# One transfer of queries a tile instead of two, in a windowed attention with two mixtures of experts behind it

## The chip, the cores and the metric

The kernel runs on one core of a Trainium2 chip. The metric is the device time in microseconds: before the change 337.52 us, the median of 3 runs (336.28 to 339.29).

A core has five engines that run side by side: TensorE (PE, matrix products, with its weight loads listed as PEld), VectorE (DVE), ScalarE (ACT), GpSimd (POOL) and SyncE (SP). SP computes nothing here: it issues transfers between the chip's memory (HBM) and the core's own memory of 128 partitions, and waits on semaphores before it issues. The transfers themselves are carried out by 16 DMA engines.

## The reference

Three stages follow one another. Batch 8, 8 heads, 576 positions, head size 64; the experts see 4608 rows of 512.

```python
scores = scale * np.matmul(q, k.transpose(0, 1, 3, 2))
mask_plain = (rel >= 0) & (rel < window)                                      # heads 0 to 3, window 32
mask_dil = (rel >= 0) & (rel < window * dilation) & (rel % dilation == 0)     # heads 4 to 7, dilation 4
attn = softmax(np.where(masks, scores, -1e9)); x = np.matmul(attn, v)
...
logits = x @ phi; d = softmax(logits, axis=0); slot_input = d.T @ x           # 32 slots, 8 experts
slot_out = relu(slot_input @ w1[e]) @ w2[e]; x = softmax(logits, axis=1) @ slot_out
...
e = argmax(x @ w_gate); out = gate * (relu(x @ m1[e]) @ m2[e])                # one expert a row
```

## The kernel before

The host lays out the inputs so that the dilated heads become plain ones: their positions are sorted by the remainder of 4. Every head then needs a window of at most 32 keys back, and a tile of 128 queries looks at its own 128 keys and the 32 before them.

The attention runs over 36 tiles (NTILE) of 128 queries, all 8 heads at once. Heads go in 4 groups `p`, and in each group two heads `hh` share the 128 partitions: head size 64 times 2 heads, interleaved, so that partition 2d + hh holds element d of head hh. `qt[t]` is `[128, 4, 128]` float32: partition, group, query. In HBM a tile's queries are 128 rows of 4 x 128 numbers (2 KB): first the 64 rows of hh = 0, then the 64 rows of hh = 1. `load` (lines 155 to 165) fetches them with two transfers of 64 rows, one to the even and one to the odd partitions (line 159), and the keys with two more (line 161) into `kt[r]`, in which the rows of one head are zero where the other head's keys stand; each row of 2 KB goes to four places of 512 B there. GpSimd then copies the last 32 keys of the tile before to the front (line 163). `load_v` (lines 174 to 185) fetches the values of a tile, 64 rows of 4160 B in each of two transfers (line 185). `load_w_part` (lines 109 to 122) fetches a part of an expert's weights, 512 KB in one transfer of 128 rows (lines 117 and 119); `prefetch` (line 127) spreads 28 of these parts over the attention's steps.

A step `s` of the loop (lines 490 to 519) sends to SP, in this order: at most one weight part as a rule, then `load(s + 2)`, which is q, q, k, k, then `load_v(s - 1)`, which is v, v. On PE a step holds the scores of tile s (`qk`, line 198, `s_ps`), the transposes of the probabilities of an earlier tile (`tr`, line 242, `a_ps`), the products with the values (`pv`, line 263, `x_ps`), the transposes of the result (`xt`, line 290), and in some steps the logits and the slot sums (`b_sl`, line 418, `sl_ps`). The first tiles' order is written out by hand (`HEAD`), and so is the end (`TAIL`). The scores of a tile need its q and both transfers of its k.

`q` and `kt` have two buffers each. So the q of tile t + 2 may be fetched only when PE has done the scores of tile t, and SP, which handles its list strictly in order, holds everything behind it meanwhile. Transfers from SP also share eight landing semaphores (DMAHW0 to DMAHW7 in the lists below) in rotation: an issue waits until the transfer eight places before it, which used the same semaphore, has landed.

After the attention come the rest of the weights for the experts, page by page as pages come free, and the two expert stages.

Of the kernel before, what the change touches and what calls it, by code (L numbers as in the profile page):

```python
# [73 lines left out]
def kernel_body(ctx, tc, q, k, v, mask, cpack, dk, rk, w1, w2, m1, m2, out):  # L74
    nc = tc.nc
# [22 lines left out]
    with tc.manual_schedule(), ExitStack() as ab:  # L98
# [34 lines left out]
        with ExitStack() as a:  # L133
# [19 lines left out]
            qt = {}  # L153

            def load(t):
                r = t % NR
                qt[t] = qp.tile([128, 4, 128], FP32, tag="q", name="q")
                for hh in range(2):
                    nc.sync.dma_start(out=qt[t][hh:128:2], in_=q[t, 64 * hh:64 * hh + 64])  # L159
                for hh in range(2):  # L160
                    nc.sync.dma_start(out=kt[r][hh:128:2, hh, :, WIN:], in_=k[t, hh])  # L161
                if t > 0:
                    nc.gpsimd.tensor_copy(  # L163
                        out=kt[r][:, :, :, 0:WIN], in_=kt[1 - r][:, :, :, 128:128 + WIN]
                    )
# [8 lines left out]
            def load_v(t):  # L174
                if t == NTILE - 2:
                    for i in range(NR):
                        for hh in range(2):
                            nc.sync.dma_start(
                                out=keys_as_values(i)[hh:128:2, hh],
                                in_=v[t, hh, :, 2 * i:2 * i + 2].rearrange("k p j c -> k (p j c)"),  # L180
                            )
                    return
                r = value_slot(t)
                for hh in range(2):
                    nc.sync.dma_start(out=vt[r][hh:128:2, hh], in_=v[t, hh])  # L185
# [7 lines left out]
            def qk(t, where="s", eng=nc.gpsimd):  # L193
                r = t % NR
                ps = psums[where].tile([128, 4, 64, 2], FP32, tag=where, name="s_ps")
                for p in range(4):
                    for j in range(4):
                        nc.tensor.matmul(  # L198
                            out=ps[32 * j:32 * j + 32, p].rearrange("q k h -> q h k"),
                            lhsT=qt[t][:, p, 32 * j:32 * j + 32],  # L200
                            rhs=kt[r][:, :, p, 32 * j:32 * j + 64],
                            start=True,
                            stop=True,
                        )
                del qt[t]
                s = sp.tile([128, 4, 64, 2], FP32, tag="s", name="s")
                first, step = MASKS[t % 9]
                for a in range(2):
                    nc.vector.tensor_tensor(  # L209
                        out=s[:, 2 * a:2 * a + 2],  # L210
                        in0=ps[:, 2 * a:2 * a + 2],
                        in1=mask_sb[:, first + a * step].unsqueeze(1).unsqueeze(3).to_broadcast([128, 2, 64, 2]),
                        op=ALU.add,
                    )
                mx = sm.tile([128, 4, 2], FP32, tag="mx", name="mx")
                nc.vector.tensor_reduce(out=mx, in_=s.rearrange("p a k h -> p a h k"), op=ALU.max, axis=AX.X)  # L216
                eng.tensor_tensor(  # L217
                    out=s, in0=s, in1=mx.unsqueeze(2).to_broadcast([128, 4, 64, 2]), op=ALU.subtract
                )
                s_sb[t] = s  # L220
# [162 lines left out]
            def b_order(b, engs="a"):  # L383

                n = 4 // len(engs)
                for k, eng in enumerate(engs):
                    r = slice(n * k, n * k + n)
                    o = lt_sb[b][:, 2, :].rearrange("p (r i) -> p i r", r=4)[:, :, r]
                    i = lt_sb[b][:, 1, :].rearrange("p (i r) -> p i r", r=4)[:, :, r]
                    copy(eng, o, i)  # L390
# [84 lines left out]
            def once(c, t, f, *o):  # L475
# [7 lines left out]
                c=lambda t: nc.sync.dma_start(out=cp_sb, in_=cpack), o=lambda t: nc.vector.memset(on_sb, 1.0),  # L483
                l=load, v=load_v, X=ex, r=tr, p=pv, x=xt,
                q=lambda t, w="s", e="g": qk(t, w, nc.gpsimd if e == "g" else nc.vector),
# [4 lines left out]
            for s in range(NTILE - 1):  # L490
# [16 lines left out]
                t = s - 4  # L507
# [20 lines left out]
            def b_lz(b):  # L528

                lt_sb[b] = tp.tile([128, 3, S], FP32, tag="lt", name="lt", bufs=1)  # L530
                mz = sm.tile([128, 2], FP32, tag="mz", name="mz", bufs=1)
                for c in range(2):
                    ps = lz_ps[c] = ps_m.tile([128, 288], FP32, tag="m", name="lt_ps")
                    nc.tensor.matmul(
                        out=ps, lhsT=is_sb, rhs=l4_sb[b][:, 288 * c:288 * c + 288], start=True, stop=True
                    )
                    nc.vector.tensor_reduce(out=mz[:, c:c + 1], in_=ps, op=ALU.max, axis=AX.X)
                mn = sm.tile([128, 1], FP32, tag="mn", name="mn")
                nc.vector.scalar_tensor_tensor(
                    out=mn, in0=mz[:, 0:1], scalar=m_run[0], in1=mz[:, 1:2], op0=ALU.max, op1=ALU.max  # L540
                )
                ng = sm.tile([128, 1], FP32, tag="ng", name="ng")
                nc.vector.tensor_scalar(out=ng, in0=mn, scalar1=-1.0, scalar2=None, op0=ALU.mult)
                ng_sb[b] = ng

            def b_ez(b):
                lt, ng = lt_sb[b], ng_sb[b]
                fac[b] = sm.tile([128, 1], FP32, tag="fac", name="fac")
                for c in range(2):
                    nc.scalar.activation(  # L550
                        out=lt[:, 1, 288 * c:288 * c + 288], in_=lz_ps[c], func=ACTF.Exp, bias=ng, accum_out=zb2[:, c:c + 1]
                    )
                nc.scalar.activation(out=fac[b], in_=m_run[0], func=ACTF.Exp, bias=ng)

            def b_zz(b):
                for c in range(2):
                    nc.scalar.activation(
                        out=zsum, in_=zsum, func=ACTF.Identity, scale=1.0 if c else fac[b], bias=zb2[:, c:c + 1]
                    )
                nc.scalar.activation(out=zsum, in_=zsum, func=ACTF.Copy, bias=1e-9)  # L560

            def b_isz():
                nc.vector.reciprocal(out=zsum, in_=zsum)
                nc.scalar.activation(out=isz, in_=is_sb[:, 0:NSLOT], func=ACTF.Copy, scale=zsum)

            def b_keep(b):
# [8 lines left out]
                q=lambda n, o: qk(last), v=lambda n, o: load_v(last - n),  # L575
# [6 lines left out]
                t=lambda n, o: b_lz(z), e=lambda n, o: b_ez(z), o=lambda n, o: b_order(z, *o),  # L582
                d=lambda n, o: b_dt(z, (n, n + 1)), z=lambda n, o: b_zz(z), i=lambda n, o: b_isz(),
# [11 lines left out]
            for h in range(2):  # L595
                o = slice(256 * h, 256 * h + 256)
                nc.vector.scalar_tensor_tensor(
                    out=acc[:, o], in0=acc[:, o], scalar=fac[z], in1=ps[:, o], op0=ALU.mult, op1=ALU.add
                )
                for c in (2 * h, 2 * h + 1):  # L600
                    nc.tensor.matmul(
                        out=si_ps[:, c], lhsT=acc[:, 128 * c:128 * c + 128], rhs=isz, start=True, stop=True
                    )
            nc.vector.tensor_copy(
                out=sm_sb.rearrange("p c (e x) -> p c e x", x=36)[:, :, :, 0:SPE],
                in_=si_ps.rearrange("p c (e s) -> p c e s", s=SPE),
# [22 lines left out]
        for p in late:  # L629
# [15 lines left out]
            out=csum[:, 0], in_=c_sb.rearrange("p t s -> p s t"), op=ALU.add, axis=AX.X  # L645
# [6 lines left out]
            out=isw[:, NSLOT:2 * NSLOT], in0=is_sb[:, 0:NSLOT], scalar1=-1.0 / NSLOT, scalar2=None, op0=ALU.add  # L652
# [84 lines left out]
        for e in range(E):  # L737
            for c in range(4):
                for j in range(4):
                    nc.tensor.matmul(  # L740
                        out=h_ps[32 * j:32 * j + 32, :],
# [25 lines left out]
        for hf in range(2):  # L767
            nc.vector.tensor_copy(
                out=hm_sb[:, hf].rearrange("p j (e x) -> p j e x", x=36)[:, :, :, 0:SPE],
                in_=ht_ps[:, hf].rearrange("p (j e s) -> p j e s", j=4, s=SPE),  # L770
# [5 lines left out]
        for e in range(E):  # L776
            for fc in range(8):
                g = fc % 4
                nc.tensor.matmul(  # L779
                    out=so_ps[32 * g:32 * g + 32, :],  # L780
# [41 lines left out]
        for c in range(4):  # L822
            nc.tensor.matmul(
                out=lb_ps, lhsT=xm[:, c:c + 1], rhs=wg_sb[:, c], start=(c == 0), stop=(c == 3)
# [16 lines left out]
        for c in range(4):  # L841
            for a in range(4):
                nc.tensor.matmul(
                    out=g_ps[32 * a:32 * a + 32, :], lhsT=st_sb[:, c], rhs=wg_sb[:, c], start=(c == 0), stop=(c == 3)
# [7 lines left out]
            out=gbd[:, 0:4], in0=g_ps.unsqueeze(1).to_broadcast([128, 4, E]), in1=bm_sb, op=ALU.mult  # L852
# [12 lines left out]
        for b in range(9):  # L865
            nc.tensor.matmul(
                out=lg_w[:, 4 * b:4 * b + 12, :], lhsT=ct(b), rhs=gbd, start=True, stop=True
# [36 lines left out]
        def small(name, shape, dtype=FP32):  # L904
# [26 lines left out]
            out=trd_bf, in0=id_sb, scalar=1664.0, in1=tri_sb, op0=ALU.mult, op1=ALU.add  # L931
# [312 lines left out]
        def pick(k):  # L1244
# [10 lines left out]
            a=across, m=mixed_of, p=pick, h=halved,  # L1255
# [79 lines left out]
        with tc.If(nrest > 0):  # L1335
            rest(tc, dict(
                out=out, rk=rk, rev_sb=rev_sb, wes=wes, eq=eq, wm=wm, on_sb=on_sb, c_sb=c_sb, gate=gate,
# [377 lines left out]
```

## Time and profile before

| | before |
|---|---|
| median of 3 runs | 337.52 us (336.28 to 339.29) |
| profiled execution: time, span of the core | 340.81 us, 339.0 us |
| busy, share of the span: PE, DVE, ACT, POOL | 82%, 61%, 49%, 25% |
| transfers in total | 87.53 MB, mean 258 GB/s |
| q transfers | 72 of 128 KB, median 4.8 us from issue to landing |
| k transfers | 72 of 128 KB, 4.3 us |
| v transfers | 70 of 260 KB, 4.7 us |
| weight parts (w) | 72 of 512 KB, 6.3 us |

All rows of the profile come from one profiled execution, whose time is a little above the median. "Busy" leaves out the issuing of transfers, so SP has no busy time; it shows as SPq in the chain of work. The chain follows the work that ended last back from the end, at each step to what released it.

### The profile page before, as it was taken

What the parts mean: (1) busy time and instruction counts of PE and PEld (TensorE: products, weight loads), DVE (VectorE), ACT (ScalarE), POOL (GpSimd) and SP (SyncE); (2) the same over time, 40 slices, a digit from 0 to 9 for tenths busy, and PEclk for the clock granted to TensorE, in tenths of its full rate; (3) what the DMA queues carried; (4) which work ended last, traced back from release to release, by engine and by line L of the source; (5) the groups of instructions that cost most, each with busy time, mean ns of one, the idle gap of its engine ahead of it and who ended that gap; (6) DMA issues with size and microseconds to landing.
All of it is one profiled execution on the core that took longest, in us unless ns stands there. A gap on an engine that the chain in (4) does not pass through costs nothing.

```text
span 339.0 us, 10076 instructions
## 1 busy us (share of the span) xinstructions
PE 278.5 (82%) x3977; PEld 192.2 (57%) x3977; DVE 207.6 (61%) x512; ACT 164.6 (49%) x379; POOL 84.3 (25%) x139
## 2 busy tenths in 40 slices
PE   2677768998789889779787889899977778999992
PEld 1555556665665656556555535544463346888871
DVE  4645537868768687586867865532028866357760
ACT  1114537565574674474844841222113485187752
POOL 4023233222522324322223003930003343000000
PEclk9959999999999999999999999999999997999998
DMA  5878899998998989999989899999567020367654
GB/s 150 269 248 260 269 318 320 279 318 278 294 337 263 297 275 298 310 294 326 302 280 310 283 364 318 384 386 386 194 205 292 2 79 14 85 149 268 245 217 161
DMA packets 53954, 87.53 MB, mean 258 GB/s; under 512 B 5584, under 2 KB 26320, under 8 KB 53904
## 3 DMA queue, kind: packets, MB, share of 16 engines
q1 hardware_dynamic: 53520, 86.06, 76.8%
q0 software_dynamic: 384, 0.79, 0.9%
q8 instruction: 33, 0.54, 0.6%
q14 instruction: 17, 0.14, 0.1%
HBM read 77.39 MB, written 9.44 MB: 256 GB/s over the span
## 4 chain that ended last, share of the span: by engine, by line
PE 45%; DMA 24%; DVE 13%; SPq 10%; issue 4%; POOL 1%; ACT 1%; POOLq 0%; DVEq 0%
DMA kt<-in_k_dram 12%; PE o_ps L1169 9%; DMA vt<-in_v_dram 7%; DMA pg<-in_moe_w_dram 5%; PE s_ps L198 5%; PE so_ps L779 4%; PE sl_ps L418 4%; PE x_ps L263 4%; SPq L159 3%; SPq L161 3%; SPq L185 3%; PE o_ps L1162 2%; DVE trb L402 2%; PE a_ps L242 2%; PE cs_ps L724 1%
## 5 line engine op out<-in xcount | busy, mean ns | idle before, releaser
L198 PE MATMUL s_ps<-kt,q 128*32 128x128 f32 x1152 | 42.3, 291 | 31.8 <-DMA kt<-in_k_dram 28.1
L198 PEld LDWEIGHTS s_ps<-kt,q 128*32 128x32 f32 x1152 | 33.0, 116 | 40.2 <-issue 28.3
L217 POOL TENSOR_TENSOR s<-s,mx 128x512 f32<-128x512 f32 x33 | 34.5, 1044 | 77.6 <-DVE mx L216 39.6
L209 DVE TENSOR_TENSOR s<-s_ps,mask_sb 128x256 f32<-128x256 f32 x72 | 27.1, 417 | 30.6 <-PE s_ps L198 28.1
L263 PE MATMUL x_ps<-vt,at 128*32 128x130 f32 x1120 | 39.1, 279 | 7.5 <-DMA vt<-in_v_dram 7.3
L237 ACT ACTIVATE l<-l_ps 64x128 f32<-64x128 f32 (+4 forms) x100 | 24.1, 287 | 35.5 <-PE l_ps L319 35.1
L263 PEld LDWEIGHTS x_ps<-vt,at 128*32 128x32 f32 x1120 | 29.8, 109 | 13.7 <-issue 10.6
L1169 PE MATMUL o_ps<-pg,pg 128*128 128x512 f32 x132 | 36.9, 395 | 0.0
L1169 PEld LDWEIGHTS o_ps<-pg,pg 128*128 128x128 f32 x132 | 25.0, 190 | 6.5 <-issue 0.8
L224 ACT ACTIVATE e<-s 128x512 f32<-128x512 f32 x36 | 22.4, 623 | 11.6 <-DVE s L217 10.6
L237 ACT ACTIVATE at<-a_ps 128x512 f32<-128x512 f32 x34 | 20.3, 598 | 13.2 <-PE a_ps L242 12.4
L237 ACT ACTIVATE xt<-t_ps 128x512 f32<-128x512 f32 x36 | 21.4, 594 | 10.3 <-PE t_ps L290 10.1
L278 DVE TENSOR_TENSOR x<-x_ps,rec 128x512 f32<-128x512 f32 (+1 forms) x38 | 25.2, 663 | 1.3
L216 DVE TENSOR_REDUCE mx<-s 128x8 f32<-128x512 f32 x36 | 24.8, 688 | 1.2
L242 PE MATMUL a_ps<-cp_sb,e 128*128 128x128 f32 x144 | 24.9, 298 | 0.7 <-ACT e L224 0.7
L290 PE MATMUL t_ps<-cp_sb,x 128*128 128x128 f32 x144 | 23.4, 284 | 0.5 <-DVE den L273 0.5
L402 DVE STREAM_TRANSPOSE trb<-lt 32x480 f32<-32x480 f32 (+3 forms) x48 | 22.5, 468 | 1.7 <-ACT lt L550 1.2
L163 POOL COPY kt<-kt 128x256 f32<-128x256 f32 x35 | 13.9, 398 | 34.2 <-DMA kt<-in_k_dram 32.8
L1118 ACT ACTIVATE pg<-o_ps,gm 128x512 f32<-128x512 f32 x22 | 15.0, 689 | 12.5 <-PE o_ps L1169 12.2
L242 PEld LDWEIGHTS a_ps<-cp_sb,e 128*128 128x128 f32 x144 | 16.0, 147 | 8.2 <-PE s_ps L198 5.2
L290 PEld LDWEIGHTS t_ps<-cp_sb,x 128*128 128x128 f32 x144 | 15.6, 140 | 7.7 <-issue 5.6
L418 PE MATMUL sl_ps<-x,trb 128*32 128x256 f32 (+1 forms) x160 | 18.4, 390 | 0.0
(264 smaller groups left out, 440.9 us busy)
## 6 DMA issues: line engine op xcount, KB each, us to landing
pg<-in_moe_w_dram SPq DMA_DIRECT2D x72, 512.0 KB, 6.3
vt<-in_v_dram SPq DMA_DIRECT2D x70, 260.0 KB, 4.7
q<-in_q_dram SPq DMA_DIRECT2D x72, 128.0 KB, 4.8
kt<-in_k_dram SPq DMA_DIRECT2D x72, 128.0 KB, 4.3
out_dram<-pg SPq DMA_DIRECT2D x28, 256.0 KB, 2.1
out_dram<-pg SPq DMA_DIRECT2D x16, 128.0 KB, 2.3
kt<-in_v_dram SPq DMA_DIRECT2D x4, 130.0 KB, 6.5
dk_sb<-in_dk_dram SPq DMA_DIRECT2D x1, 370.5 KB, 10.3
```

The source lines that it names most:

```text
L198: nc.tensor.matmul(out=ps[32 * j:32 * j + 32, p].rearrange("q k h -> q h k"), lhsT=qt[t][:, p, 32 * j:32 * j + 32], rhs=kt[r][:, :, p, 32 ...
L209: nc.vector.tensor_tensor(out=s[:, 2 * a:2 * a + 2], in0=ps[:, 2 * a:2 * a + 2], in1=mask_sb[:, first + a * step].unsqueeze(1).unsqueeze(3 ...
L216: nc.vector.tensor_reduce(out=mx, in_=s.rearrange("p a k h -> p a h k"), op=ALU.max, axis=AX.X)
L217: eng.tensor_tensor(out=s, in0=s, in1=mx.unsqueeze(2).to_broadcast([128, 4, 64, 2]), op=ALU.subtract)
L237: nc.scalar.activation(out=out, in_=in_, func=ACTF.Copy)
L242: nc.tensor.transpose(ps[:, p], e_sb[t][:, p], id_sb)
L263: nc.tensor.matmul(out=ps[32 * j:32 * j + 32, p // 2 - sl.start, o:o + 2 * VW], lhsT=at_sb[t][:, p, 32 * j:32 * j + 32], rhs=vt[r][:, :, p ...
L278: nc.vector.tensor_tensor(out=x_sb[t][:, sl], in0=pv4[:, :, :, 0:HD], in1=rec.to_broadcast([128, n, 4, HD]), op=ALU.mult,)
L290: nc.tensor.transpose(ps[:, p], xf[:, p * 128:(p + 1) * 128], id_sb)
L402: nc.vector.transpose(out=tr_sb[b // 2][p0:p0 + 32, ws[0]:ws[1], i0:i0 + n, :], in_=src)
L418: nc.tensor.matmul(out=ps[32 * g:32 * g + 32, 256 * w:256 * w + 256], lhsT=tr_sb[b // 2][r0:r1, 1 + w, t % 9, :], rhs=xf[r0:r1, 256 * w:25 ...
L1169: nc.tensor.matmul(out=outs[b, i], lhsT=l[:, 128 * i:128 * i + 128], rhs=r, start=False, stop=(c == last and m == len(xs[b, c]) - 1),)
```

## The change

The two transfers of 64 rows become one of 128 rows. On the side of the core's memory it fills the partitions 0, 1, 2, ... in order; on the HBM side its rows come alternately from the first and the second half of the tile's 128 rows (d outside, h inside). The same bytes end in the same places. The key transfers stay two.

```diff
             def load(t):
                 r = t % NR
                 qt[t] = qp.tile([128, 4, 128], FP32, tag="q", name="q")
-                for hh in range(2):
-                    nc.sync.dma_start(out=qt[t][hh:128:2], in_=q[t, 64 * hh:64 * hh + 64])
+                nc.sync.dma_start(
+                    out=qt[t].rearrange("p a c -> p (a c)"), in_=q[t].rearrange("(h d) a c -> d h (a c)", h=2)
+                )
                 for hh in range(2):
                     nc.sync.dma_start(out=kt[r][hh:128:2, hh, :, WIN:], in_=k[t, hh])
```

Only SP's list changes. In the loop, a tile's share of that list with a weight part ahead and behind, before the change (a row is one issue: line, what it writes and reads, rows and shape, and the semaphores it waits on; the number behind a name is a buffer's):

```order
L117 DMA pg_543<-in_moe_w_dram 128x1024 [waits DMAHW6_49]
L159 DMA q<-in_q_dram 64x512 [waits DMAHW7_49,PE_49]
L159 DMA q<-in_q_dram 64x512 [waits DMAHW0_49]
L161 DMA kt_117<-in_k_dram 64x4x128 [waits DMAHW1_49,Pool_49]
L161 DMA kt_117<-in_k_dram 64x4x128 [waits DMAHW2_49]
L185 DMA vt_118<-in_v_dram 64x1040 [waits DMAHW3_49,PE_49]
L185 DMA vt_118<-in_v_dram 64x1040 [waits DMAHW4_49]
L117 DMA pg_543<-in_moe_w_dram 128x1024 [waits DMAHW5_49]
L159 DMA q<-in_q_dram 64x512 [waits DMAHW6_49,PE_49]
```

The last row's q waits on DMAHW6, which is the semaphore of the weight part in the first row. The same place in SP's list after the change (lines behind the edit stand one further down, those ahead of it are the same):

```order
L117 DMA pg_534<-in_moe_w_dram 128x1024 [waits DMAHW5_49]
L158 DMA q<-in_q_dram 128x1x512 [waits DMAHW6_49,PE_49]
L162 DMA kt_117<-in_k_dram 64x4x128 [waits DMAHW7_49,Pool_49]
L162 DMA kt_117<-in_k_dram 64x4x128 [waits DMAHW0_49]
L186 DMA vt_118<-in_v_dram 64x1040 [waits DMAHW1_49,PE_49]
L186 DMA vt_118<-in_v_dram 64x1040 [waits DMAHW2_49]
L117 DMA pg_534<-in_moe_w_dram 128x1024 [waits DMAHW3_49]
L158 DMA q<-in_q_dram 128x1x512 [waits DMAHW4_49,PE_49]
L162 DMA kt_116<-in_k_dram 64x4x128 [waits DMAHW5_49,Pool_49]
```

There are six issues from one q to the next instead of seven, and the semaphore of the weight part in the first row, DMAHW5, is now waited on by the first k of the next tile instead of its first q.

At the start of the program SP's list is, before the change:

```order
L159 DMA q<-in_q_dram 64x512 x2
L161 DMA kt_116<-in_k_dram 64x4x128 [waits DVE_49]
L161 DMA kt_116<-in_k_dram 64x4x128
L482 DMA mask_sb<-in_mask_dram 128x768
L159 DMA q<-in_q_dram 64x512 x2
L161 DMA kt_117<-in_k_dram 64x4x128 [waits Pool_49]
L161 DMA kt_117<-in_k_dram 64x4x128 [waits DMAHW0_49]
L483 DMA cp_sb<-in_cpack_dram 128x456 [waits DMAHW1_49]
```

and after it:

```order
L158 DMA q<-in_q_dram 128x1x512
L162 DMA kt_116<-in_k_dram 64x4x128 [waits DVE_49]
L162 DMA kt_116<-in_k_dram 64x4x128
L483 DMA mask_sb<-in_mask_dram 128x768
L158 DMA q<-in_q_dram 128x1x512
L162 DMA kt_117<-in_k_dram 64x4x128 [waits Pool_49]
L162 DMA kt_117<-in_k_dram 64x4x128
L484 DMA cp_sb<-in_cpack_dram 128x456
```

Each tile's q takes one place in the list where it took two, and the first waits on landing semaphores come two places further on in the work.

## Rows read from the trace of the kernel before

**Rows 1.** The page's part on the chain that ended last, by engine.

```profile
PE 45%; DMA 24%; DVE 13%; SPq 10%; issue 4%; POOL 1%; ACT 1%; POOLq 0%; DVEq 0%
```

**Rows 2.** Busy time of each engine by stretch of the span; columns in its head.

```profile
core 0: us, PE busy (x) PEld busy (x) DVE busy (x) ACT busy (x) POOL busy (x), PEclk, DMA share, GB/s
0.00:20.00 20.00, 8.10 (x144) 6.54 (x147) 11.25 (x19) 2.54 (x3) 4.75 (x10) 0.88 0.75 222
20.00:182.00 162.00, 135.72 (x2736) 97.77 (x2728) 111.39 (x269) 93.13 (x224) 51.31 (x83) 0.98 0.91 293
...
140.00:180.00 40.00, 35.07 (x692) 24.75 (x692) 29.89 (x73) 24.20 (x57) 12.57 (x21) 1.00 0.95 303
...
212.00:240.00 28.00, 26.02 (x283) 13.87 (x287) 10.64 (x26) 5.87 (x12) 10.20 (x10) 1.00 1.05 385
```

**Rows 3.** Waits of PE, 20 to 182 us: total us, times, longest.

```profile
PE s_ps L198 <- DMA kt<-in_k_dram: 16.2, 15, 1.9
PE x_ps L263 <- DMA vt<-in_v_dram: 4.9, 7, 1.1
```

**Rows 4.** Issues of lines 159 and 161: duration min/median/max in ns.

```profile
L159 SPq DMA_DIRECT2D q<-in_q_dram x72: 471/590/1287, 0.9 to 170.4; - x72
...
L161 SPq DMA_DIRECT2D kt<-in_k_dram x72: 558/606/1247, 2.3 to 172.0; - x72
```

**Rows 5.** The chain, 0 to 24 us: start, length, what.

```profile
1.20 1.14 DVE kt L467
...
3.62 0.60 SPq L482
...
4.80 0.60 SPq L159
...
13.14 0.59 SPq L159
...
14.40 0.04 issue
14.44 4.97 DMA kt<-in_k_dram
```

**Rows 6.** SP in order of time, 59 to 82 us: start, length, issues of line 159.

```profile
60.60 1.76 SPq L159 DMA_DIRECT2D q<-in_q_dram  x2
...
65.90 1.71 SPq L159 DMA_DIRECT2D q<-in_q_dram  x2
...
71.53 1.11 SPq L159 DMA_DIRECT2D q<-in_q_dram  x2
...
75.66 1.19 SPq L159 DMA_DIRECT2D q<-in_q_dram  x2
```

**Rows 7.** The chain, 64 to 84 us.

```profile
65.01 6.46 DMA pg<-in_moe_w_dram
...
71.53 0.47 SPq L159
...
73.35 4.14 DMA kt<-in_k_dram
...
77.62 1.08 PE s_ps L198 x32
```

**Rows 8.** Waits of SP, 20 to 182 us: total us, times, longest.

```profile
SPq L159 <- DMA pg<-in_moe_w_dram: 6.5, 14, 0.8
```

**Rows 9.** Waits of SP over the whole span.

```profile
SPq L119 <- PE sl_ps L418: 8.6, 2, 5.0
```

**Rows 10.** Transfers, 20 to 182 us: count, KB each, median us to landing.

```profile
pg<-in_moe_w_dram SPq DMA_DIRECT2D x25, 512.0 KB, 5.9
q<-in_q_dram SPq DMA_DIRECT2D x62, 128.0 KB, 4.8
kt<-in_k_dram SPq DMA_DIRECT2D x62, 128.0 KB, 4.4
```

**Rows 11.** Transfers, 0 to 20 us.

```profile
kt<-in_k_dram SPq DMA_DIRECT2D x10, 128.0 KB, 3.3
```

## The prediction

> **What bounds the kernel now.** I read the chain that ended last first. By engine [rows 1] it is PE 45%, DMA 24%, SPq 10%: a fourth of the span is the landing of a transfer, and a tenth is SyncE's queue doing nothing but issuing transfers. Next, the table by stretch [rows 2], to see where that happens. The attention loop is the stretch 20 to 182 us: PE is busy 135.72 of 162 us, and the DMA engines have a share of 0.91 at 293 GB/s. The weight stream behind the loop (212 to 240 us) has 1.05 at 385 GB/s, so in the loop the DMA engines are close to full but not full. Within the loop, 140 to 180 us had 0.95 at 303 GB/s.
>
> Then the waits of PE inside the loop [rows 3]: 16.2 us for keys (15 times) and 4.9 us for values (7 times), 21.1 us together. That is the ceiling of anything that only makes loads arrive sooner.
>
> Then what SP does. One issue of q takes 590 ns in the median, one of k 606 ns [rows 4], though one moves only 128 KB: at the 385 GB/s of [rows 2] that is 131,072 / 385 = 0.34 us of DMA work. Values (260 KB, 0.69 us by the same rate) take about as long to move as to issue, a weight part (512 KB, 1.36 us) longer. A tile with a weight part is q q k k v v w: seven issues. With 0.04 us between issues (the piece at 14.40 us in [rows 5]), seven cost some 4.4 us; the tiles that I looked at follow one another at 60.60, 65.90 and 71.53 us, so 5.3 and 5.6 us, and 71.53 to 75.66 = 4.1 us where no weight part lies between [rows 6].
>
> The difference is in the order. SP's waits go round eight landing semaphores (DMAHW0 to DMAHW7), so that an issue waits until the eighth transfer before it has landed. In a tile of seven the one that waits for the weight part is the first q. The chain shows it: the weight part issued at 65.01 lands 6.46 us later, at 71.47, the first q stands at 71.53, the last k at 73.35, which lands after 4.14 us, and the scores start at 77.62 [rows 7]. Over the loop that wait is 6.5 us in 14 times [rows 8].
>
> Behind the loop nothing runs free of it: SP's weight parts after attention wait 8.6 us for the slot sums on PE [rows 9], which end the attention, so that stream moves with the loop's end.
>
> **What the change does, step by step.** It removes 36 transfers of 128 KB and makes 36 others 256 KB. Bytes stay, rows stay 2 KB, PE, DVE, ACT and POOL keep their instructions and order.
>
> *Price of the new issue.* The trace has no q issue of 128 rows with an alternating source. Nearest rows: 590 ns (q, 64 rows) and 606 ns (k, four pieces a row) [rows 4], and the mask's transfer of 128 rows, which the chain of the start lists at 0.60 us [rows 5]. I take 0.60 us. So the saving on SP is 0.59 + 0.04 = 0.63 us a tile, 36 x 0.63 = 22.7 us of SP time. Bounds: if the issue took 1.2 us the saving would be nothing; 0.56 us would add 1 us in all.
>
> *Start (0 to 20 us).* Here SP issues without a stop and the chain lies on it [rows 5]. The first tile saves nothing: the chain lies there on the memset of kt, 1.20 + 1.14 = 2.34 us, for which its first k waits, and not on q. In tiles 1 to 3 the second q (the first of three at 4.80, the last at 13.14 us, 0.59 to 0.60 us each, with 0.04 us behind it) falls out of the chain that ends in the k issued at 14.44: 3 x 0.63 = 1.9 us. The DMA share of 0.75 [rows 2] lets most of this through. Bounds: 0 and 1.9 us; I take 1.9.
>
> *Loop.* 32 further issues are gone, 32 x 0.63 = 20.2 us of SP time. What of it reaches the end? In a tile with a weight part the semaphore rule gives a floor. Before: the first q may go when the weight part issued just ahead of the previous first q has landed, so q to q is at least its landing time less one issue, 5.9 - 0.63 = 5.3 us (5.9 us is the median in [rows 10]); that is what [rows 6] show. After: six transfers a tile, so the eighth back of the first q is a v, and the wait for the weight part falls on the first k, one issue later than q: 5.9 - 1.26 = 4.6 us. On 25 weight parts [rows 10] this is 25 x 0.63 = 16 us if the landing time stayed at 5.9.
>
> It will not stay. A landing time is mostly queue: k landed in 4.4 us in the loop and in 3.3 us in the start [rows 10, 11], where the share is 0.75. Sooner issue lengthens the queue wherever the DMA engines are already busy; only their idle time can be won. Idle is 0.09 x 162 = 14.6 us by a full share of 1.00, and 162 - 0.91 x 162 / 1.05 = 21.6 us by the share of the stream. So the loop's gain lies between 0 (every earlier issue only queues) and 14.6 to 21 us. For a value I take the pace that this mix of transfers already reached in its best stretch: all 162 us at 303 instead of 293 GB/s, 162 x (1 - 293/303) = 5.3 us. Eight transfers in flight then hold 8/6 instead of 8/7 of a tile, which is what should feed the DMA engines through the weaker stretches.
>
> *Cost of packets.* 128 rows of 2 KB as before, on DMA work, zero; 36 completion marks fewer, under 1 us. What late q costs: both halves were needed by the first score matmul before, so one landing for both delays nothing.
>
> *Sum.* 1.9 + 5.3 = 7.2 us off the profiled execution's 340.81 us (339.0 us span and 1.8 us around it) gives 333.6; that execution is 3.3 us above the median of the runs, 337.52. From the median: 330.3 us.
>
> **Rivals.**
> *A, the time is hidden (no change).* The DMA engines' work sets the loop's pace, or SP's saved time turns into waits for buffers: q has two buffers, and the q of tile t+2 must wait for the scores of tile t on PE; behind that wait on SP stand k and v. For it: share 0.91, landing times of 4.4 to 5.9 us, well above the start's 3.3 [rows 10, 11]. Against: PE waits 21.1 us for loads [rows 3] and the best stretch runs faster. Only the start's 1.9 us is left: 335.6 us. The Trainium skill ("DMA: Bandwidth & Descriptors", section "Issuing engines are not separate DMA queues") says that the sequencer's time to start a DMA is usually small beside the DMA itself, which speaks for this rival; the trace disagrees for these transfers, 0.59 us of issue [rows 4] against 0.34 us of work. By that rule the loop's term would be nothing.
>
> *B, all of the idle is won.* Share 1.00 through the loop: 14.6 + 1.9 = 16.5 us, 321.0 us. For it: SP has 20.2 us less to do, PE waits 21.1 us. Against: the best 40 us have 0.95 [rows 2], and PE is busy 135.72 of 162 us, so a loop of 147 us leaves it hardly a gap.
>
> *C, slower.* The source alternates between places 128 KB apart, row by row. If that made reading q slower, or put the transfer on fewer DMA engines, DMA work grows in a loop that is short of it. By bytes, q is 62 x 128 KB of 47.4 MB (162 us at 293 GB/s), 17%, so 17% of 0.91 x 162 = 25 us of work. At half the pace that is 25 us more, of which idle takes up at most 14.6: +10 us in the loop, 337.5 + 10 - 1.9 = 346 us. It decides from where the extra work exceeds what I count as gain plus 1%, 7.2 + 3.4 = 10.6 us, which is q at 42% more per byte. For it: nothing but that no row shows the pattern. Against: k, whose rows fall into four pieces of 512 B, lands as fast as q (4.4 and 4.8 us) [rows 10]. The Trainium skill (same page, section "Why a DMA increments its semaphore by 16 and not by 1") lets a transfer use the largest number up to 16 that divides the outer sizes of both sides, here 128 and 64, so 16 engines and no loss; no run here shows it.
>
> That the change does not do what it says is no rival: SP's list has one q issue a tile.
>
> **How the numbers follow.** About 1% (3.4 us) is what a measurement of this kernel can tell from no change, so the borders are 334.1 and 340.9. The forecast (326 to 334.1 us) has 0.48, B and what lies towards it (under 326) 0.15, A 0.27, C 0.10. Faster is 0.48 + 0.15 = 0.63, same 0.27, slower 0.10. The range takes in nearly all of B and A, and what leaves C out: 322 to 338 us. The forecast's own range is 326 to 334.
>
> **What would show it.** Right: q issues at 0.6 us in the new profile, 36 of them; the chain's SPq share down from 10%; the first long score wait in the start ended by a k issued near 12.5 instead of 14.44 us; SP's wait for a weight part now in front of k; 20 to 182 us shrunk by about 5 us at about 303 GB/s; PE's wait for keys down from 16.2 to about 11 us. A shows as the same GB/s with k's landing time above 4.4 us, or longer waits of the q line for PE. C shows as a higher DMA share at no more GB/s. The prediction is wrong if the issue of the merged transfer costs over 0.8 us, or if loads already come as fast as the DMA engines can bring this mix.

## The result, and the profile after

The changed kernel took 328.35 us, the median of 4 runs (327.36 to 334.72). The kernel before took 338.4 us beside it (median of 4, 336.28 to 339.4). The ratio is 0.97, with a 95% interval of 0.9631 to 0.9768: 3% faster. Runs over 1.5% above the fastest of their kernel, such as the one of 334.72 us, are left out of the ratios here. The forecast was 330.3 us. The sign, the place and the chain of causes came out as forecast; the gain in the loop was larger than its term.

The profiled executions are 340.81 us before and 328.09 us after, with spans of 339.0 and 326.3 us. That difference of 12.7 us is larger than the 10.05 us between the medians, because the profiled execution of before lay some 2 to 3 us above the medians of its kernel (337.52 and 338.4 us), and that of after did not.

The chain that ended last, by engine, for the changed kernel:

```profile
PE 61%; DVE 11%; DMA 10%; ACT 9%; issue 3%; SPq 3%; POOL 1%; DVEq 0%; POOLq 0%
```

Against [rows 1], the landing of transfers went from 24 to 10% of the span, SP's issuing from 10 to 3%, and PE from 45 to 61%. The chain has left SP's list and runs mostly through matrix work.

Busy time by stretch, changed kernel (columns in the head). The loop's last scores now end near 167 us instead of 179, so the loop is read from 20 to 171 us, where [rows 2] have 20 to 182:

```profile
core 0: us, PE busy (x) PEld busy (x) DVE busy (x) ACT busy (x) POOL busy (x), PEclk, DMA share, GB/s
0.00:20.00 20.00, 9.96 (x168) 8.13 (x168) 11.96 (x22) 2.94 (x4) 4.83 (x10) 1.00 0.77 233
20.00:171.00 151.00, 135.26 (x2741) 97.18 (x2742) 111.48 (x272) 93.13 (x225) 51.35 (x83) 0.99 0.96 316
140.00:170.00 30.00, 28.34 (x587) 19.67 (x580) 23.46 (x58) 18.14 (x43) 10.06 (x18) 1.00 0.93 306
```

The same PE work (135.26 us against 135.72) fits into 151 us instead of 162. The DMA engines move 316 GB/s instead of 293, at a share of 0.96 instead of 0.91.

Waits of PE, 20 to 182 us (total us, times, longest), which answer to [rows 3]:

```profile
PE s_ps L199 <- DMA kt<-in_k_dram: 8.4, 6, 2.4
...
PE x_ps L264 <- DMA vt<-in_v_dram: 0.4, 1, 0.4
```

Keys went from 16.2 to 8.4 us, values from 4.9 to 0.4: of 21.1 us of waiting for loads, 12.3 are gone. Waits of SP in the same stretch, which answer to [rows 8]:

```profile
SPq L158 <- PE l_ps L320: 16.0, 17, 2.1
...
SPq L162 <- DMA pg<-in_moe_w_dram: 2.5, 5, 0.8
```

The wait for a weight part has moved from q's line (6.5 us, 14 times) to k's (2.5 us, 5 times). A new first row has appeared: SP stands at q for 16.0 us because PE has not yet done with the older of q's two buffers. (The releaser's name is the last PE work before; q's buffer is what the issue needs. One case: the scores that start at 78.40 us end at 79.46, and the q that takes their buffer goes out at 79.56.)

Transfers, 20 to 171 us, changed kernel (count, KB each, median us to landing), which answer to [rows 10]:

```profile
pg<-in_moe_w_dram SPq DMA_DIRECT2D x26, 512.0 KB, 6.1
kt<-in_k_dram SPq DMA_DIRECT2D x62, 128.0 KB, 4.9
q<-in_q_dram SPq DMA_DIRECT2D x30, 256.0 KB, 5.4
```

The medians of k (4.9 instead of 4.4 us) and of weight parts (6.1 instead of 5.9) are longer than before, and yet PE waits less. On the whole, then, transfers were issued earlier by more than they landed later.

### The profile page after: what moved, and what is told of

Its sections match the earlier page's. It is cut to its first block, busy times and chain, and to the rows that moved or that the text cites. A ratio compares the mean times of both kernels' runs of the same rounds, so it can differ in the third digit from the quotient of the medians.

```text
span 326.3 us, 10036 instructions
## 1 busy us (share of the span) xinstructions
PE 280.2 (86%) x3977; PEld 192.2 (59%) x3977; DVE 207.3 (64%) x512; ACT 164.5 (50%) x379; POOL 84.0 (26%) x139
## 2 busy tenths in 40 slices
DMA packets 53378, 87.53 MB, mean 268 GB/s; under 512 B 5008, under 2 KB 25744, under 8 KB 53328
## 3 DMA queue, kind: packets, MB, share of 16 engines
q1 hardware_dynamic: 52944, 86.06, 78.6%
## 4 chain that ended last, share of the span: by engine, by line
PE 61%; DVE 11%; DMA 10%; ACT 9%; issue 3%; SPq 3%; POOL 1%; DVEq 0%; POOLq 0%
PE o_ps L1170 9%; DMA kt<-in_k_dram 8%; PE x_ps L264 7%; PE s_ps L199 7%; PE sl_ps L419 6%; PE so_ps L780 5%; PE a_ps L243 4%; PE h_ps L741 4%; PE t_ps L291 3%; PE o_ps L1163 2%; ACT lt L238 2%; PE l_ps L320 2%; DMA pg<-in_moe_w_dram 2%; PE lt_ps L344 2%; SPq L162 2%
```

## The experiments

Each edit is shown by its main lines, shortened where `...` stands. e1, e6, e8, e10 and e12 to e15 are edits of the changed kernel; e2, e7 and e9 are edits of the kernel before, whose q transfers they replace. Two theories were to be told apart for the loop. One says that SP's time counts: an issue fewer lets every later issue of the tile go sooner. The other says that landing semaphores count: with six transfers in a tile instead of seven, the eighth transfer back is an older one. The rivals left over from the prediction were the new pattern of rows and a merged transfer that is itself better for the DMA engines. Ratios are to the kernel before, run beside each, with 95% intervals.

**The time back, the count not (e1).** SP's 0.6 us of a second issue is put back as a read of one number into a register, with no transfer:

```diff
+            one_i = fx.tile([1, 1], I32, name="one_i")
+            nc.gpsimd.memset(one_i, 1)
...
                 nc.sync.dma_start(out=qt[t]..., in_=q[t]...)
+                nc.values_load(one_i[0:1, 0:1], engines=[mybir.EngineType.SP], min_val=0, max_val=2)
```

> The change stays in (one q transfer of 256 KB a tile, six transfers a tile with a weight part), but SP loads a register and tests it behind each q issue, 36 times, work that takes SP some 0.7 us (the one such load at 246.18 us of the trace of before took 0.48 us and the steps behind it 0.18 and 0.03 us), which is about what the second q issue took, 0.63 us, and that issues nothing and holds no landing semaphore. If SP's time is what the change won, nearly all of it is lost again: 336 to 341 us, scores waiting for keys about 16 us in the loop as before. If the landing semaphores (eight transfers that hold 8/6 of a tile and not 8/7) are what it won, the time stays near the changed kernel's 328 us (up to 331). In between: both have a share.

335.26 us; ratio 0.9887 (0.9826 to 0.9948). The interval lies apart from that of the change (0.9631 to 0.9768). So SP's time alone takes back about two thirds of the gain, 1.9 of 3.0 points, without any transfer (2.6 of 3.8 beside the second measurement of the change, e11 below). SP in order of time in this kernel (start, length, what):

```profile
88.10 0.56 SPq L160 DMA_DIRECT2D q<-in_q_dram  x1
89.35 1.22 SPq L165 DMA_DIRECT2D kt<-in_k_dram  x2
```

From the end of q to the first k it is 89.35 - 88.66 = 0.69 us, where the changed kernel, when nothing holds its k, has about 0.1. That makes some 0.60 us a tile. The two longest waits of SP, 20 to 170 us, and PE's wait for keys, 20 to 182 us:

```profile
SPq L160 <- PE l_ps L323: 5.2, 8, 1.2
SPq L165 <- POOL s L221: 3.0, 7, 0.6
```

```profile
PE s_ps L202 <- DMA kt<-in_k_dram: 7.6, 7, 2.8
```

SP's wait at q fell from 16.0 to 5.2 us. Of some 31 x 0.60 = 18.6 us put into the loop, 10.8 us thus went into time in which SP would have stood at q anyway. The scores of the last tile end 5.2 us later than in the changed kernel. And no wait for a weight part is left in the list: with six transfers a tile and SP's time back, the semaphore does not stop SP in this run. One thing in e1 has no like in the kernel before: the read, and the write of its number on POOL, delay the first tile too, whose scores start at 6.54 us (5.88 with the change, 5.63 before). So up to 0.7 us of its loss, 0.2 points, is not the second issue's.

**The count back too (e10).** A small transfer with two buffers of its own instead of the register read: the same time on SP (1.30 us from q to k against 1.25 in e1), but seven issues and seven semaphores a tile.

```diff
+                nc.sync.dma_start(out=scr[t % 2], in_=q[t, 0:16, 0, 0:64])
```

> As the run with one small transfer behind each q issue, but with two buffers for it in turn (16 rows of 256 B), so that it waits for no earlier small transfer, only for its turn of the landing semaphores: seven issues and seven semaphores in a tile with a weight part, as before the change, with the queries in one transfer. Beside the register load (the same SP time, six semaphores, ratio 0.989) the difference is the semaphore alone and next to no bytes. If the semaphores have a share of the gain: ratio 1.000 to 1.010, no better than before. If only SP's time has: 0.985 to 0.993. The earlier form's ratio of 1.018 would then be its wait for its own buffer.

341.77 us; ratio 1.0053 (1.0001 to 1.0105). The whole gain is gone, with q still one transfer of 128 rows. Against e1, which costs SP the same, it is 1.7% slower, and the intervals do not touch. Its SP waits and PE waits, 20 to 170 and 20 to 182 us:

```profile
SPq L159 <- DMA pg<-in_moe_w_dram: 5.1, 7, 1.3
```

```profile
PE s_ps L201 <- DMA kt<-in_k_dram: 22.1, 18, 2.7
```

The wait for the weight part is back in front of q. What differs from e1 is the eighth place in the rotation, and a transfer of 4 KB a tile with its own work for the DMA engines.

**A first form of it that misled (e6).** One buffer for the small transfer instead of two.

```diff
+                nc.sync.dma_start(out=scr, in_=q[t, 0:16, 0, :])
```

> The change stays in, and behind each q issue stands one more small transfer (16 rows of 512 B, 8 KB, into a buffer that nobody reads): the count of issues and of landing semaphores is that of before, the queries still come in one transfer of 128 rows, and the DMA engines get 1 packet of 512 B each more a tile, some 0.03 us. If the count of issues is the cause (SP's time, semaphores, or both), all of the gain is lost: 336 to 341 us. If the form of the transfer (128 partitions in order) or less DMA work is the cause, it stays near 328 us. Beside the run with the register load it gives the semaphores' share: what this one is slower than that one.

343.52 us; ratio 1.0181 (1.0055 to 1.0307, from three runs), slower than the kernel before. Its waits of SP show a likely reason: the small transfer waited for its own predecessor, a wait that before does not have, so its excess says nothing on the count.

```profile
SPq L162 <- DMA scr<-in_q_dram: 7.2, 12, 1.3
```

**Two transfers over all partitions (e9).** As many transfers as before, each over 128 partitions with the change's alternating source, half a row (1 KB) each:

```diff
+                for g in range(2):
+                    nc.sync.dma_start(
+                        out=qt[t][:, 2 * g:2 * g + 2].rearrange("p a c -> p (a c)"),
+                        in_=q[t].rearrange("(h d) a c -> d h (a c)", h=2)[:, :, 256 * g:256 * g + 256],
+                    )
```

> Two q transfers a tile over all 128 partitions with the alternating source, split by head groups (two groups each: 128 rows of 1 KB, 128 KB a transfer). Issues and landing semaphores are as before, the pattern is that of the change; the DMA engines have 16 rows of 1 KB where they had 8 of 2 KB a tile each, some 0.06 us a tile more by the packets of 1 KB in the traces. If the count of issues is the cause: as before, ratio 0.995 to 1.015, scores waiting some 16 to 20 us for keys in the loop. If the pattern is: ratio 0.97 to 0.98.

339.75 us; ratio 1.0036 (0.9981 to 1.0091), no change against the kernel before. Busy time by stretch, and SP's wait for a weight part at q, 20 to 182 us:

```profile
20.00:170.00 150.00, 124.75 (x2511) 91.28 (x2508) 102.62 (x246) 87.07 (x210) 46.74 (x73) 0.97 0.92 292
```

```profile
SPq L159 <- DMA pg<-in_moe_w_dram: 2.8, 5, 0.8
```

That is the pace of before (0.91 and 293 GB/s in [rows 2]). So the pattern and the width of the transfer do not bring the gain without the count. (Its rows of 1 KB could hide a small gain of the pattern; the expectation puts their price at some 2 us in all.)

**Two transfers of 64 neighbouring partitions (e2).** This too was meant to have before's count with the change's source:

```diff
+                for hh in range(2):
+                    nc.sync.dma_start(
+                        out=qt[t][64 * hh:64 * hh + 64].rearrange("p a c -> p (a c)"),
+                        in_=q[t].rearrange("(h d) a c -> d h (a c)", h=2)[32 * hh:32 * hh + 32],
+                    )
```

> Two q transfers of 64 rows a tile again, but each with the changed kernel's pattern: 64 neighbouring partitions (0 to 63, 64 to 127), source rows alternating between the heads. If the number of issues is the cause: as before, 336 to 341 us. If the pattern (neighbouring partitions instead of every second one, alternating source) is the cause: near 328 us. A time above 341 us would say that the pattern costs something that the single transfer hid.

349.7 us; ratio 1.035 (1.0225 to 1.0475, from three runs). Busy time by stretch, and q's transfers from 20 to 170 us:

```profile
20.00:170.00 150.00, 122.02 (x2404) 88.79 (x2399) 96.42 (x231) 81.84 (x197) 45.40 (x71) 0.97 0.98 280
```

```profile
q<-in_q_dram SPq DMA_DIRECT2D x58, 128.0 KB, 5.4
```

Over this stretch the DMA engines are busier than in any other kernel here (0.98) and move less (280 GB/s). Part 3 of each run's profile page says the same: the packets of SP's queue took 80.5% of a span of 344.7 us, 277.5 us an engine, where those of the kernel before, as many and with the same bytes, took 76.8% of 339.0 us, 260.4. So this is slower data movement, which e9 (76.5% of 339.9 us, 260.0) and the change (78.6% of 326.3 us, 256.5) do not have, and the run cannot speak on the count. Its cause was not pursued.

**Half of it (e7).** Even tiles merged, odd tiles as before: 18 issues fewer instead of 36.

```diff
+                if t % 2 == 0:
+                    nc.sync.dma_start(out=qt[t]..., in_=q[t]...)
+                else:
+                    for hh in range(2):
+                        nc.sync.dma_start(out=qt[t][hh:128:2], in_=q[t, 64 * hh:64 * hh + 64])
```

> Dose: only the even tiles' queries come in one transfer, the odd tiles' in two of 64 rows, so 18 issues are gone and not 36. If each removed issue is worth about the same: half of the gain, about 333 us (331 to 335). If there is a threshold (SP is the last to be waited for until it has some slack, and nothing is won behind that), more than half of the gain comes with the first 18: 329 to 331 us. If the gain hangs on the landing semaphore's turn (first k and not first q waits for the weight part), less than half.

333.41 us; ratio 0.978 (0.9618 to 0.9941, from three runs). It lies between, at 306 GB/s from 20 to 170 us. The interval is too wide to say whether half the issues bring half the gain or more.

**More issues fewer (e8).** The attention's weight parts in pairs, 1 MB in one transfer: 14 further issues gone.

```diff
+            if i < E and wpos[0] < 2 * NW:
+                if sub == 0:
+                    nc.sync.dma_start(
+                        out=wt[i, hf].rearrange("p (a f) -> p a f", a=2),
+                        in_=src[e, part * 128:(part + 2) * 128, :].rearrange("(a p) f -> p a f", p=128),
+                    )
```

> The change, and in the attention the weight parts in pairs: 1 MB in one transfer where two of 512 KB stood, 14 issues fewer. If the loop is still short of SP's time, 14 x 0.63 = 9 us more of it are free and a third to a half of that shows: 324 to 326 us (ratio 0.955 to 0.965). If SP now waits for PE anyway and the keys queue behind a weight part (1 MB is 2.7 us of DMA work at 385 GB/s): no gain or a loss, ratio 0.97 to 0.985.

340.23 us; ratio 1.0019 (0.9969 to 1.007). All of the gain is lost, with fewer issues than ever. Waits of PE in the loop, the weight transfers from 20 to 170 us, and a wait of SP there:

```profile
PE s_ps L205 <- DMA kt<-in_k_dram: 14.4, 9, 3.9
```

```profile
pg<-in_moe_w_dram SPq DMA_DIRECT2D x12, 1024.0 KB, 8.0
```

```profile
SPq L168 <- DMA pg<-in_moe_w_dram: 7.4, 8, 1.7
```

The longest wait for keys is 3.9 us instead of 2.4 with the change. Two things speak for the 1 MB as the cause: it lands after 8.0 us, so that keys issued right behind it share the DMA engines with it for longer, and SP itself, in the last fence, waits 7.4 us at k's line until it has landed (2.5 us with the change). The run does not tell the two apart. A third thing goes with them: the granted clock over 20 to 170 us was 0.95, with the change 0.99, and a matmul of the scores took 289 ns in the mean instead of 279. It may follow from PE's longer waits; that was not tested. What the run shows is that fewer issues did not help here, with 1 MB put ahead of what PE waits for.

**Weight parts from another engine (e12).** The attention's weight parts are issued by POOL, so SP's tile has five issues.

```diff
+                (nc.gpsimd if wpos[0] < 2 * NW else nc.sync).dma_start(
+                    out=o, in_=src[e, part * 128:(part + 1) * 128, :]
+                )
```

> The change, and the attention's 28 weight parts are issued by POOL instead of SP: SP has five issues in every tile, 28 x 0.63 = 17.6 us of its time are free, and the eight landing semaphores of SP serve q, k and v alone. If SP's time or the semaphores still bind the loop: some us faster than the changed kernel, ratio 0.95 to 0.965. If SP already waits for PE's buffers, as its waits in the changed kernel's trace say (16.0 us on one line): no gain, ratio 0.97; a loss if the weight parts, no longer held back by SP's order, get ahead of the keys in the DMA engines, or if POOL pays for the issue in front of the subtraction that PE's next steps need: ratio above 0.98.

337.42 us, the median of four runs (333.2 to 340.21). The lower two, 333.2 and 335.0 us, are the ones to compare, too few for a ratio. They lie below every run of the kernel before beside them (336.16 to 347.88) and above all four of the change (e11 below, 324.34 to 327.02): no gain over the change, but a loss. In its one profile SP stands still longer at q (23.3 us, 20 times, against 16.0), and PE waits for keys up to 4.2 us and for values again:

```profile
PE s_ps L201 <- DMA kt<-in_k_dram: 8.9, 8, 4.2
PE x_ps L266 <- DMA vt<-in_v_dram: 7.6, 5, 2.6
```

Tile by tile, the scores of the 27th tile start when they do with the change (123.90 against 123.88 us), and those of the 29th 3.48 us later (136.03 against 132.55). In between POOL issued three weight parts within 4 us (at 125.06, 126.99 and 128.90 us), and one transfer of keys among them, issued at 127.69 us, took 8.21 us to land. Behind the scores of the last tile another 2.7 us were lost (162.7 us to the end of the span against 160.0). So up to the 27th tile the time freed on SP beyond the change's brought nothing, and the loss in the loop came where weight parts, no longer held by SP's order, ran beside the keys.

**The change again (e11).**

> The changed kernel once more, as the mark for the runs beside it on the same chip: ratio to before 0.96 to 0.98 by every theory.

326.59 us (324.34 to 327.02); ratio 0.9623 (0.9533 to 0.9714). Its loop ran at 321 GB/s and a share of 0.97.

**Three tries to go on from the change (e13, e14, e15).** e13 issues the mask and the constants from ACT, and the constants earlier, so that the start of SP's list is shorter (its edit is shown; the order of `HEAD` is not). e14 puts the weight part behind q and k instead of ahead of them. e15 does both.

```diff
-                k=clear_k, z=clear_v, m=lambda t: nc.sync.dma_start(out=mask_sb, in_=mask),
-                c=lambda t: nc.sync.dma_start(out=cp_sb, in_=cpack), o=lambda t: nc.vector.memset(on_sb, 1.0),
+                k=clear_k, z=clear_v, m=lambda t: nc.scalar.dma_start(out=mask_sb, in_=mask),
+                c=lambda t: nc.scalar.dma_start(out=cp_sb, in_=cpack), o=lambda t: nc.vector.memset(on_sb, 1.0),
```

> The change, and the mask's and the constants' transfers are issued by ACT, which is idle then, so that SP's list of the start has two issues fewer, 1.25 us. If the start lies on SP's issues, 1.2 us less than the changed kernel: ratio some 0.004 below its 0.962 to 0.970 (hard to tell from it by time); the trace should show the first long score waits end about 1.2 us sooner.

> The change, and a step's weight part is issued behind the step's q and k and ahead of its v, instead of ahead of q. If what is left of PE's waits for keys (6 to 8 us in the loop of the changed kernel) is the weight part queued ahead of them (1.3 us of DMA work), they shrink and the time falls by 2 to 5 us: ratio 0.95 to 0.96. If v has no slack, the waits go over to the values: ratio 0.96 to 0.975.

> Both of the last two edits together. If both gain: ratio 0.945 to 0.957, faster than the changed kernel. If the weight part's place gains nothing: as the start alone, 0.958 to 0.967.

e13: 326.62 us, ratio 0.963 (0.9566 to 0.9695). e14: 328.67 us, 0.9674 (0.9605 to 0.9743). e15: 328.82 us, 0.9711 (0.9625 to 0.9798). None can be told from the change (0.97 and 0.9623). In e14 the wait only changed its owner, by PE's waits in the loop:

```profile
PE x_ps L264 <- DMA vt<-in_v_dram: 9.9, 11, 2.3
PE s_ps L199 <- DMA kt<-in_k_dram: 3.1, 3, 1.8
```

Keys fell from 8.4 to 3.1 us and values rose from 0.4 to 9.9. In e13 PE's wait for keys in the first 20 us is 8.9 us against 9.6 with the change: two issues fewer stand in front of the third tile's keys, but the last of these went out at 9.23 us, only 0.19 us sooner than with the change (9.42), because that tile's q had to wait for the first tile's scores to end at 7.93 us; and it took 4.50 us to land instead of 4.19.

## Why the prediction was right, and where it was off

*The price of the new issue* was right. Taken at 0.60 us, it is 556/562/1444 ns (minimum, median, maximum) on the new line; the first row is q's and the second k's, in the form of [rows 4]:

```profile
L158 SPq DMA_DIRECT2D q<-in_q_dram x36: 556/562/1444, 0.9 to 157.2; - x36
```

```profile
L162 SPq DMA_DIRECT2D kt<-in_k_dram x72: 547/600/1547, 2.3 to 158.5; - x72
```

A transfer of twice the rows cost SP no more than one half did (562 against 590 ns), and the 4 KB of e10 cost it 590 ns too.

*The start's term*, 1.9 us, came nearly true at the place where it was counted, and did not last. Scores of the fourth and fifth tile, changed kernel and kernel before (PE in order of time: start, length, what, and in brackets the idle time ahead):

```profile
17.89 1.08 PE L199 MATMUL s_ps<-kt,q 128*32 128x128 f32 x32 [0.77 <-DMA kt<-in_k_dram]
...
22.00 1.08 PE L199 MATMUL s_ps<-kt,q 128*32 128x128 f32 x32 [2.44 <-DMA kt<-in_k_dram]
```

```profile
19.55 1.94 PE L198 MATMUL s_ps<-kt,q 128*32 128x128 f32 x32 [2.50 <-DMA kt<-in_k_dram]
...
22.58 1.94 PE L198 MATMUL s_ps<-kt,q 128*32 128x128 f32 x32
```

Those of the fourth tile start 1.66 us sooner. The last k for them is the second of the pair that SP began at 12.07 us, so at about 12.68, forecast as 12.5, instead of 14.44 [rows 5]. Those of the fifth start only 0.58 us sooner: its q, at 15.74 us, had to wait for the third tile's scores (13.74 to 15.72 us), whose buffer it takes, and its last k, issued at 16.99 us, took 4.87 us to land. The prediction named this wait under rival A and left it out of the start's sum. By the sixth tile the lead is 2.62 us (25.21 against 27.83), so how much of it is the start's depends on the tile at which one cuts.

*The loop's term*, 5.3 us, is the step that was mis-sized. The last scores show it, changed kernel and before:

```profile
166.30 1.08 PE L199 MATMUL s_ps<-kt,q 128*32 128x128 f32 x32
```

```profile
178.36 1.08 PE L198 MATMUL s_ps<-kt,q 128*32 128x128 f32 x32
```

They come 12.06 us sooner; less the start's 1.66 us, that is 10.4 us in the loop, nearly twice the term (11.5 us if one cuts at the fifth tile). From the start of the last scores to the end of the span the two kernels take about the same, 160.6 us before and 160.0 after, so the gain lies in the attention. By the medians it is less, about 10.05 - 1.66 = 8.4 us, since the two profiles exaggerate; it is still over 1.5 times the term. The step took the best stretch of the kernel before (303 GB/s) as the pace that the whole loop would come to. But that stretch stood under the same seven issues and semaphores as the rest, so it did not show what the DMA engines can do with this mix. The changed kernel has 316 GB/s over 151 us, and e11 has 321. The bound of 14.6 us, from idle to a share of 1.00, held, and the time came out between the forecast and rival B.

*The split of cause* was argued in the prediction with both parts, the time and the semaphores, and did not size them apart. The runs do: e1 puts SP's time back and loses 1.9 points of 3.0; e9 and e10 have the count of before as well and lose the rest. So of a gain of 3 to 3.8% some 1.9 to 2.6 is SP's time, and the seventh transfer is worth 1.1 (from e1 to the kernel before) to 1.7 (1.5 between e1 and e9, 1.7 between e1 and e10).

That this second part is the rotation, and not something else that a seventh transfer brings, is argued and not shown. For it speaks the list of waits: for the weight part at q 5.1 us in e10, none in e1. In e9 that wait is smaller, 2.8 us, so this link is the weaker one. A rival is the work of the DMA engines themselves, which the profile pages let one size, by share and span as under e2: 260.4 us an engine before, 256.5 with the change, 258.9 in e1 (78.1% of 331.5 us), 260.0 in e9 and 262.3 in e10 (76.8% of 341.6 us). The change and e1 have the same transfers and differ by 2.4 us, so differences of that size go with the timing. Of the 1.7 points of e10 some may be its 3.4 us more of this work than e1; of e9's 1.5 points (5 us) its 1.1 us more can explain little.

Where e1's 5.2 us stand on PE is only in part known. About 1.5 us were lost in the start, where SP issues without a stop (the fourth tile's scores start at 19.35 us, with the change at 17.89). Its wait for keys in the loop is 7.6 us against 8.4, and the rest of the loss is spread over small waits.

*The semaphore's move* came as forecast: the wait for a weight part passed from q to the first k, and shrank from 6.5 to 2.5 us.

*Rival A* fell on the time, but its mechanism is there: SP waits at q for PE, 16.0 us in 17 times, and landing times are longer. This is what stands next: in e8 and e12, which save SP further issues, SP's wait for PE at q rose to 21.7 and 23.3 us, so a good part of what SP saved there (14 x 0.63 = 8.8 and 28 x 0.63 = 17.6 us) it spent at q's two buffers. That more buffers would win it back was not tried.

The Trainium skill ("DMA: Bandwidth & Descriptors", section "Issuing engines are not separate DMA queues"), which the prediction set against the trace, calls the sequencer's time to start a DMA usually small beside the DMA itself. By that rule the loop's term would have been nothing. Beside the time to landing the issue is small here too (0.56 us against 5.4 for q), but the issues follow one another on SP, and 0.60 us more of SP's time a tile, with no transfer behind it, cost 1.9 points (e1). So the measurement decides against what the prediction drew from it for this list. The Trainium skill (same page, section "Rules for kernel authors") advises one transfer over 128 partitions instead of two to disjoint halves. The result agrees (0.97), though e9 shows that the gain here is in the count and not in the width.

*Rival B* (321.0 us) came half true: a share of 0.96, not 1.00. The prediction says that its range, 322 to 338 us, takes in nearly all of B, but B's own time lies outside it. *Rival C* fell: q lands at the pace of its neighbours (5.4 us for 256 KB beside 4.9 for 128 KB of k), and the loop moves more GB/s, not less. Its border, q at 42% more per byte, leaves out the 14.6 us of idle that the same paragraph lets the extra work fill.

*Cost of packets* was put at under 1 us and left out of the sum. The pages of the two profiles count 5584 packets under 512 B before and 5008 after, 576 fewer, which is 16 for each of the 36 transfers that are gone. No run prices them alone; the packets' time fell by 3.9 us an engine with the change and by 1.5 us in e1, so the term may have been more than 1 us.

*What would show it* held in all points but the loop's length and rate, which went past the forecast: keys at 8.4 us where about 11 were expected, 316 GB/s where 303 were.

## What to carry to other kernels

Where one engine issues all loads, count its issues: compare the time of an issue with the time that its bytes need (here 0.59 against 0.34 us), and where the issue is the longer, try to merge what has the same readers. The pace of the best stretch is not a ceiling when that stretch waits on the same thing that the change takes away; here the gain lay between that pace and the idle share of the DMA engines. Be careful with merging a transfer that nobody waits for when small urgent loads stand behind it (e8), and where the issuing engine already waits for buffers.

## What was not expected of the hardware

Two transfers of 64 neighbouring partitions with 2 KB rows (e2) cost 3.5% against the kernel before, at a DMA share of 0.98 and 280 GB/s; two transfers over every second partition (before) or over all 128 (e9) ran at 0.91 to 0.92 and 292 to 293 GB/s with the same bytes. And 14 issues fewer, with 1 MB ahead of the keys instead of 512 KB, cost the whole gain of the change (e8): such a transfer landed in a median of 8.0 us against 6.1.
